# Sign bits of most weight blocks moved from VectorE to ScalarE, and attention blocks ordered earlier, in a fused attention and two-layer kernel

## The chip, the cores and the metric

The kernel runs on one core of one Trainium2 chip. Five engines share the work: TensorE (PE, with its weight loads shown as PEld), VectorE (DVE), ScalarE (ACT), GpSimd (POOL) and SyncE (SP), which here issues all DMAs. The metric is device microseconds (us) of one execution. The kernel before took 1275.98 us in the median of 3 runs (1275.0 to 1279.07).

## What is computed

```
scores = q @ k.T / sqrt(64)                  # 4 batches x 8 heads, 576 x 64 each
keep the 32 largest of each row of 576, softmax over these, attn @ v
x   = rows of the batches, 2304 x 512        # heads side by side
x   = (sigmoid(x @ w_gate) * (x @ w_val)) @ w_out      # 512 -> 1536 -> 512
out = relu(x @ w_in)**2 @ w_out2                       # 512 -> 2048 -> 512
```

q, k and v arrive in float32. All five weights arrive in float64, which no engine computes with: each value is two 32-bit words in SBUF, and the kernel makes a float32 of them by itself.

## The kernel before, in words

The 2304 rows are cut into 18 tiles of 128, and these into 12 chunks (`CHUNKS`): six of one tile, then six of two. For each chunk, attention runs over units: one unit is one tile and one head, with scores on TensorE, a copy `S` to SBUF by ScalarE (L376), four rounds of the eight largest by VectorE (MAX8 L388 and MATCH_REPLACE8 L395), two ScalarE passes for the softmax (L407, L423), a transposition and the product with v. A chunk of one tile has 8 units. Its result is `x_plain` for the first two chunks (L540), which then go through both layers in float32 (`moe32`), straight on the float32 weights. Later chunks use weights and inputs split into two float16 parts.

The weights are worked on while the first attention units run. They come as 68 blocks of 128 x 512 (the names `wg`, `wv`, `wo`, `wi` and `w2`, the last printed as `w` in some rows), two blocks in a step, so 34 steps, each one call of `conv`. For one block of a step: ScalarE copies the high word, taken as float32, times a power of two into `c` (L606); VectorE shifts `c` left by 3, once for both blocks (L620), and ors the sign bit of the high word `hi` into it (L621); ScalarE turns the low word into a small integer in place (L625); and GpSimd adds that integer to `c` (L626). Then the raw block's buffer is free, and SyncE can issue the load of a later block (L579). When the last step of a weight is done, TensorE and VectorE take its scale (L643 to L652).

The order of the work comes from priorities, which a scheduler uses when it lists the instructions of each engine. In the last part of the kernel function two counters are kept: `tw` for weight steps (3 units each, `CW`) and `ta` for attention units (6 units each, `CA`, later 5). The smaller one goes next. `ta` starts at `CA0`. When `x_plain` of a chunk is listed, the body of `moe32` follows, and it forces the weight steps it needs ahead of it. Each engine then works through its list strictly in order.

```python
tw, ta, tm = 0.0, CA0, None
...
            elif tw <= ta and nstep[0] < len(steps):
                at(tw)
                weight_step()
                tw += CW
```

Of the kernel before, what the change touches and what calls it, by code (L numbers as in the profile page):

```python
# [8 lines left out]
F16 = mybir.dt.float16  # L9
BF16 = mybir.dt.bfloat16  # L10
F32 = mybir.dt.float32
F32R = mybir.dt.float32r
I32 = mybir.dt.int32
U32 = mybir.dt.uint32
AF = mybir.ActivationFunctionType
ALU = mybir.AluOpType
# [12 lines left out]
CHUNKS = [[0], [1], [2], [3], [4], [5]] + [[i, i + 1] for i in range(6, 18, 2)]  # L29
AHEAD = 1000  # L30
LEAD = 10
CA0 = -5.0
CA = 6.0
CW = 3.0
SUP = -100.0
# [12 lines left out]
SM2 = ()  # L48
XUP = 1000
DIAG = 2  # L50
SGN = 0
M4RAW = 0
KEYS1 = 1
SWI = 5
# [19 lines left out]
def tile_topk_attention__then__two_moe_layers(  # L74
# [14 lines left out]
    nc = tc.nc  # L89
# [469 lines left out]
    nblk = [0]  # L559
# [5 lines left out]
    def fetch_to(i):  # L565
        while fetched[0] < len(blocks):
            b = fetched[0]
            spare = b >= len(blocks) - M4RAW
            if b > i and not (b <= i + PREF and (spare or live[0] + 3 <= WSLOTS)):
                break  # L570
            n, kt, fb = blocks[b]
            src = weights[n][kt * P : (kt + 1) * P, fb * 512 : (fb + 1) * 512]
            pool, kw = (mpool, {"tag": "m4", "bufs": M4}) if spare else (wpool, {"tag": "w"})
            if src.dtype == F32:
                t = pool.tile([P, 512], F32, name=f"{n}_r{kt}_{fb}", **kw)
                nc.sync.dma_start(t, src)
            else:
                t = pool.tile([P, 512, 2], U32, name=f"{n}_r{kt}_{fb}", **kw)
                nc.sync.dma_start(t.rearrange("p f t -> p (f t)"), src.bitcast(U32))  # L579
            if not spare:  # L580
                live[0] += 1
            raws[(n, kt, fb)] = t
            fetched[0] += 1

    def conv(name, pi):

        pr = pairs_of[name][pi]
        fetch_to(blocks.index((name, *pr[-1])))
        if (name, pi) in CM4:
            c = mpool.tile([P, 2, 512], F32, tag="m4", bufs=M4, name=f"{name}_c{pi}")  # L590
        else:
            c = wpool.tile([P, 2, 512], F32, tag="w", name=f"{name}_c{pi}")
            live[0] += 1
        rs = [raws.pop((name, kt, fb)) for kt, fb in pr]
        ci = c.bitcast(U32)
        wide = weights[name].dtype != F32
        for e, r in enumerate(rs):
            nblk[0] += 1
            if not wide:
                nc.gpsimd.tensor_copy(c[:, e], r)  # L600
            elif YMOD and nblk[0] % YMOD == 0:
                nc.gpsimd.tensor_scalar(
                    c[:, e], r.bitcast(F32)[:, :, 1], REBIAS, 1.0, op0=ALU.mult, op1=ALU.mult
                )
            else:
                nc.scalar.activation(c[:, e], r.bitcast(F32)[:, :, 1], AF.Copy, scale=REBIAS)  # L606
        if wide:
            for e, r in enumerate(rs):
                hi = r[:, :, 1]
                if SGN and nblk[0] % SGN == 0:  # L610

                    nc.gpsimd.tensor_scalar(
                        hi.bitcast(F32), hi.bitcast(F32), 0.0, 1.0, op0=ALU.mult, op1=ALU.mult
                    )
                    nc.vector.scalar_tensor_tensor(
                        ci[:, e], ci[:, e], 3, hi, op0=ALU.logical_shift_left, op1=ALU.bitwise_or
                    )
                else:
                    if e == 0:
                        nc.vector.tensor_scalar(ci, ci, 3, None, op0=ALU.logical_shift_left)  # L620
                    nc.vector.scalar_tensor_tensor(  # L621
                        ci[:, e], hi, 0x80000000, ci[:, e], op0=ALU.bitwise_and, op1=ALU.bitwise_or
                    )
                low = r[:, :, 0].bitcast(I32)
                nc.scalar.activation(low, r[:, :, 0], AF.Copy, scale=float(2.0**-29))  # L625
                nc.gpsimd.tensor_tensor(  # L626
                    c.bitcast(I32)[:, e], c.bitcast(I32)[:, e], low, op=ALU.add
                )
        live[0] -= sum(blocks.index((name, *b)) < len(blocks) - M4RAW for b in pr)
        for e, (kt, fb) in enumerate(pr):  # L630
            flat[(name, kt, fb)] = (c, e)
# [42 lines left out]
    def weight_step(n=1):  # L674
        for _ in range(min(n, len(steps) - nstep[0])):
            name, pi = steps[nstep[0]]
            conv(name, pi)
            nstep[0] += 1
            if name in ("wg", "wv", "wo") and pi == len(pairs_of[name]) - 1:
                scale(name)  # L680
# [508 lines left out]

    tw, ta, tm = 0.0, CA0, None  # L1190
    up[0] = AUP * 50
# [95 lines left out]
```

## Time and profile before

| what | value |
|---|---|
| median of 3 runs | 1275.98 us |
| the profiled execution's own time | 1279.65 us |
| its span, first to last instruction | 1276.8 us |
| PE busy | 1185.2 us, 93% |
| DVE busy | 974.5 us, 76% |
| POOL busy | 848.8 us, 66% |
| ACT busy | 805.8 us, 63% |
| mean granted TensorE clock | 0.959 of full |

Busy time is the time in which an engine had at least one instruction under way. A share over the whole span hides the stages: an engine that is full in one stage and idle in another looks half used. So the stages have to be read apart, by windows of time, and in each the question is which engine was never idle and what the others waited for. Two instructions of one engine can overlap, so what one more costs is the distance between two starts, which is less than its duration.

### The profile page before, as it was taken

The page shows a single profiled execution, that of the slowest core. Times are in us where ns is not written, and L with a number is a line of the kernel's source. Part 1 is how long each engine was busy: PE and PEld are TensorE (multiplying, and loading weights), DVE is VectorE, ACT ScalarE, POOL GpSimd, SP SyncE. Part 2 cuts the span into 40 slices and gives each one's busy share as a digit, 9 for nine tenths or more (in the row PEclk, how much of TensorE's full clock was granted, in tenths as well). Part 3 has the DMA queues.
Part 4 walks back from the last instruction along what each step waited for, and adds up shares of the span by engine and source line. Part 5 has one row for each costly group of instructions (what it writes and reads, how often), then busy time and mean ns, then how long its engine had stood idle before and what let it go on. Part 6 is the DMA issues. An engine that isn't in the chain of part 4 may idle for free.

```text
span 1276.8 us, 30674 instructions
## 1 busy us (share of the span) xinstructions
PE 1185.2 (93%) x11477; PEld 962.5 (75%) x11477; DVE 974.5 (76%) x1989; ACT 805.8 (63%) x1695; POOL 848.8 (66%) x1294
## 2 busy tenths in 40 slices
PE   6757799989899998999998999999999999999998
PEld 5635688887787976878786768877886887787775
DVE  6999989899878968879997789999999969210010
ACT  4876766577767766767766766776676757323122
POOL 1788865477666567786875977798678749515223
PEclk9766899999989989999998999999999999999999
DMA  7977772222444336665566465566444623200000
GB/s 189 347 280 257 265 224 64 73 68 76 135 119 118 89 93 149 140 158 124 125 134 155 115 149 135 120 138 144 113 99 89 129 48 67 55 1 1 17 1 17
DMA packets 243188, 153.92 MB, mean 121 GB/s; under 512 B 193120, under 2 KB 209504, under 8 KB 243040
## 3 DMA queue, kind: packets, MB, share of 16 engines
q1 hardware_dynamic: 243040, 151.97, 46.1%
q8 instruction: 90, 1.47, 0.5%
q14 instruction: 58, 0.48, 0.1%
HBM read 105.51 MB, written 18.09 MB: 97 GB/s over the span
## 4 chain that ended last, share of the span: by engine, by line
PE 58%; DVE 17%; DMA 8%; POOL 6%; issue 5%; ACT 4%; SPq 3%; POOLq 0%; DVEq 0%; ACTq 0%
PE ph L856 11%; PE acc L877 10%; PE pg L752 6%; DVE mx L388 6%; PE pv L752 6%; DVE W L395 6%; PE acc L792 5%; PE sp L373 5%; PE xp L505 2%; PE xp L532 2%; PE ph L957 2%; PE acc L974 2%; DMA PT<-S 2%; POOL S L453 1%; DMA kst<-ks 1%
## 5 line engine op out<-in xcount | busy, mean ns | idle before, releaser
L388 DVE MAX8 mx<-W 128x8 f32<-128x576 f32 x432 | 327.8, 759 | 11.0
L395 DVE MATCH_REPLACE8 W<-mx,W 128x576 f32<-128x576 f32 x288 | 213.8, 742 | 0.0
L856 PE MATMUL ph<-x,wi_w 128*128 128x256 f16 (+1 forms) x1920 | 192.6, 255 | 2.4 <-ACT x L830 1.6
L877 PE MATMUL acc<-w_w,rh 128*128 128x512 f16 x768 | 183.1, 381 | 2.2 <-POOL rh L869 2.2
L856 PEld LDWEIGHTS <-wi_w 128*128 128x128 f16 x1920 | 158.3, 99 | 29.5 <-issue 3.0
L752 PE MATMUL pg<-xs,wg_w 128*128 128x256 f16 (+1 forms) x1440 | 150.8, 253 | 3.2 <-POOL xs L520 1.2
L752 PE MATMUL pv<-xs,wv_w 128*128 128x256 f16 (+1 forms) x1440 | 146.6, 254 | 6.2 <-DVE th L764 5.7
L373 PE MATMUL sp<-kst,qt 128*128 128x288 f32 x608 | 137.1, 336 | 11.1 <-DMA kst<-ks 5.5
L407 ACT ACTIVATE W<-S,mx 128x576 f32<-128x576 f32 x144 | 111.7, 775 | 45.8 <-DVE mx L388 45.3
L453 POOL TENSOR_TENSOR S<-W,S 128x512 f16<-128x512 f32 x192 | 137.0, 736 | 1.5
L376 ACT COPY S<-sp 128x576 f32<-128x576 f32 x144 | 91.7, 637 | 70.0 <-PE sp L373 54.7
L752 PEld LDWEIGHTS <-wv_w 128*128 128x128 f16 x1440 | 119.6, 99 | 20.9 <-issue 7.9
L752 PEld LDWEIGHTS <-wg_w 128*128 128x128 f16 x1440 | 117.8, 99 | 20.7 <-issue 3.5
L792 PEld LDWEIGHTS <-wo_w 128*128 128x128 f16 x1440 | 119.7, 99 | 16.6 <-issue 4.0
L877 PEld LDWEIGHTS <-rh 128*128 128x128 f16 x768 | 72.8, 98 | 73.9 <-POOL rh L869 2.4
L764 DVE TENSOR_TENSOR th<-pv,th 128x512 f32<-128x512 f32 (+1 forms) x60 | 34.5, 575 | 120.6 <-PE pv L752 117.5
L388 DVE MAX8 mx<-S 128x8 f32<-128x576 f32 x144 | 107.2, 744 | 20.2 <-ACT S L376 19.8
L451 POOL TENSOR_SCALAR W<-W,rz 128x576 f32<-128x576 f32 x96 | 71.8, 748 | 66.0 <-ACT S L450 63.2
L373 PEld LDWEIGHTS sp<-kst,qt 128*128 128x128 f32 x608 | 94.0, 198 | 22.2 <-DMA kst<-ks 6.7
L792 PE MATMUL acc<-gh,wo_w 128*128 128x256 f16 (+1 forms) x1104 | 107.8, 252 | 2.7 <-POOL gh L768 2.4
L868 POOL TENSOR_TENSOR r<-r 128x512 f32<-128x512 f32 (+1 forms) x80 | 69.5, 870 | 57.2 <-ACT rh L867 56.6
L395 DVE MATCH_REPLACE8 W<-mx,S 128x576 f32<-128x576 f32 x144 | 106.9, 742 | 0.0
(285 smaller groups left out, 2316.6 us busy)
## 6 DMA issues: line engine op xcount, KB each, us to landing
kst<-ks SPq DMA_DIRECT2D x112, 288.0 KB, 3.1
v<-vd SPq DMA_DIRECT2D x32, 320.0 KB, 3.4
qn<-in_q_dram SPq DMA_DIRECT2D x128, 64.0 KB, 2.4
wi_r<-in_moe_w_in_dram SPq DMA_DIRECT2D x16, 512.0 KB, 7.2
w_r<-in_moe_w_out_dram SPq DMA_DIRECT2D x16, 512.0 KB, 4.3
v<-in_v_dram SPq DMA_DIRECT2D x56, 128.0 KB, 2.3
wg_r<-in_moe_w_gate_dram SPq DMA_DIRECT2D x12, 512.0 KB, 6.3
wv_r<-in_moe_w_val_dram SPq DMA_DIRECT2D x12, 512.0 KB, 7.7
```

Source lines behind the costliest of these rows:

```text
L373: nc.tensor.matmul(sp[:, e, 0:HALF], l, r, start=(x == 0), stop=(x == len(ops) - 1))
L376: nc.scalar.copy(ss.rearrange("p (e s) -> p e s", e=2), sp[:, :, 0:HALF])
L388: m8 = nc.vector.max(mx[:, r], cur)
L395: nc.vector.match_replace(wk, mx[:, r], cur, NEG)
L407: nc.scalar.activation(wk, ss, AF.Prelu, bias=kth, scale=-1.0, alpha=1.0 / BIG)
L451: nc.gpsimd.tensor_scalar(wk, wk, rz, 1.0, op0=ALU.mult, op1=ALU.mult)
L453: nc.gpsimd.tensor_tensor(pp[:, o : o + e - f], wk[:, f:e], pp[:, f:e], op=ALU.subtract)
L752: nc.tensor.matmul(pp[:, e * N : (e + 1) * N], wblk(wd, a, c, f0, P), xs[:, b_, c, :], start=(e == 0 and n == 0), stop=(n == 3 * KM - 1), ...
L792: nc.tensor.matmul(accs[d // 2][:, (d % 2) * N : (d % 2 + 1) * N], wblk("wo", a, f, d * P, P), gh[:, b_, e * N : (e + 1) * N], start=(f == ...
L856: nc.tensor.matmul(ph[:, e * N : (e + 1) * N], wblk("wi", a, c, f0, P), x2[:, b_, c, :], start=(e == 0 and n == 0), stop=(n == 3 * KM - 1) ...
L868: nc.gpsimd.tensor_tensor(r, r, r, op=ALU.mult)
L877: nc.tensor.matmul(acc2[i][:, 0:DM], gh[:, b_, e * N + i * P : e * N + (i + 1) * P], wblk("w2", a, f, 0, DM), start=(f == 0 and x == 0), s ...
```

## The change

Of every three steps, two take another way for the sign. `nblk[0] // 2 % 3` is the step's number, counted from 1, modulo 3, and where it is 0 or 1 ScalarE writes the sign: it multiplies `hi`, taken as float32, by 2 to the power of -60 and stores the result as float16 in the upper half of the low word. The value is too small for float16, so what is stored is a zero with the sign of `hi`, and its one bit is the top bit of the word. The integer add by GpSimd, which is there anyway, carries it into `c`. The or of VectorE is not done in these steps. In the other third it is as before. The shift by VectorE now stands first in the step, and the low word's ScalarE pass stands ahead of the sign.

The second part is one number: `CA0`, from -5 to -15. With 6 units for an attention block, three attention blocks are listed ahead of the first weight step where one was.

```diff
-CA0 = -5.0
+CA0 = -15.0
...
-SGN = 0
+SGN = 3
+SGNS = (0, 1)
...
         if wide:
+            nc.vector.tensor_scalar(ci, ci, 3, None, op0=ALU.logical_shift_left)
             for e, r in enumerate(rs):
                 hi = r[:, :, 1]
-                if SGN and nblk[0] % SGN == 0:
-
-                    nc.gpsimd.tensor_scalar(
-                        hi.bitcast(F32), hi.bitcast(F32), 0.0, 1.0, op0=ALU.mult, op1=ALU.mult
-                    )
-                    nc.vector.scalar_tensor_tensor(
-                        ci[:, e], ci[:, e], 3, hi, op0=ALU.logical_shift_left, op1=ALU.bitwise_or
-                    )
+                low = r[:, :, 0].bitcast(I32)
+                nc.scalar.activation(low, r[:, :, 0], AF.Copy, scale=float(2.0**-29))
+                if nblk[0] // 2 % SGN in SGNS:
+
+                    nc.scalar.activation(
+                        r.bitcast(F16)[:, :, 1], hi.bitcast(F32), AF.Copy, scale=float(2.0**-60)
+                    )
                 else:
-                    if e == 0:
-                        nc.vector.tensor_scalar(ci, ci, 3, None, op0=ALU.logical_shift_left)
                     nc.vector.scalar_tensor_tensor(
                         ci[:, e], hi, 0x80000000, ci[:, e], op0=ALU.bitwise_and, op1=ALU.bitwise_or
                     )
-                low = r[:, :, 0].bitcast(I32)
-                nc.scalar.activation(low, r[:, :, 0], AF.Copy, scale=float(2.0**-29))
                 nc.gpsimd.tensor_tensor(
                     c.bitcast(I32)[:, e], c.bitcast(I32)[:, e], low, op=ALU.add
                 )
```

(The branch with `nc.gpsimd.tensor_scalar` was never taken before, since `SGN` was 0.)

What this does to the lists is seen at three places. In the changed kernel the lines from 51 to the high word's copy stand one further down, and those behind `conv` three further up; the high word's copy is L607, the shift L609, the low word L613, the sign L616 and the or L620 there. A number at the end of a name is a buffer's or a block's.

The first place is VectorE while `wo` is converted and the last unit of the first chunk and the first of the second are searched. Before:

```order
L620 TENSOR_SCALAR wo_c_872<-wo_c_872 128x1024
L388 MAX mx_7_933<-W_7_932 128x8
L621 SCALAR_TENSOR_TENSOR wo_c_872<-wo_r_0_720,wo_c_872 128x512
L621 SCALAR_TENSOR_TENSOR wo_c_872<-wo_r_0_722,wo_c_872 128x512
L428 RECIPROCAL rz_6_789<-bs_6_785 128x1
L620 TENSOR_SCALAR wo_c_954<-wo_c_954 128x1024
L395 MATCH_REPLACE W_7_932<-mx_7_933,W_7_932 128x576
```

Now:

```order
L396 MATCH_REPLACE W_0_974<-mx_0_975,W_0_974 128x576
L389 MAX mx_0_975<-W_0_974 128x8
L609 TENSOR_SCALAR wo_c_996<-wo_c_996 128x1024
L396 MATCH_REPLACE W_0_974<-mx_0_975,W_0_974 128x576
L389 MAX mx_0_975<-W_0_974 128x8
L609 TENSOR_SCALAR wo_c_1032<-wo_c_1032 128x1024
L620 SCALAR_TENSOR_TENSOR wo_c_1032<-wo_r_0_862,wo_c_1032 128x512
L620 SCALAR_TENSOR_TENSOR wo_c_1032<-wo_r_0_864,wo_c_1032 128x512
```

The step on `wo_c_996` has the shift alone, the next one the two ors as before. At this place attention is one unit further than it was. VectorE's list has 1559 rows before and 1513 now, 46 fewer.

The second place is ScalarE around the copy of the fourth head pair's part of `x_plain`, with which the first chunk's input is complete and its first layer can begin. Before, it is row 152 of the list:

```order
L606 ACTIVATE wi_c_1353<-wi_r_0_1152 128x512
L625 ACTIVATE wi_r_0_1152<-wi_r_0_1152 128x512
L606 ACTIVATE wi_c_1353<-wi_r_0_1154 128x512
L625 ACTIVATE wi_r_0_1154<-wi_r_0_1154 128x512
L540 COPY x_plain<-xp_3_1004 128x128
L606 ACTIVATE wi_c_1367<-wi_r_1_1248 128x512
```

Now it is row 186:

```order
L613 ACTIVATE wi_r_1_1250<-wi_r_1_1250 128x512
L607 ACTIVATE wi_c_1479<-wi_r_1_1349 128x512
L613 ACTIVATE wi_r_1_1349<-wi_r_1_1349 128x512
L607 ACTIVATE wi_c_1479<-wi_r_1_1351 128x512
L541 COPY x_plain<-xp_3_962 128x128
L613 ACTIVATE wi_r_1_1351<-wi_r_1_1351 128x512
L616 ACTIVATE wi_r_1_1248<-wi_r_1_1248 128x512
L172 CAST kp_1_1047<-kpt_1_0_1048 128x512
```

The 34 more rows ahead of it are 29 signs (L616), four copies of high words of `wi` and one softmax pass of a later unit.

The third place is ScalarE around the first Relu of the first chunk's second layer, `r_0`. Before, it is row 258:

```order
L474 COPY PT_5_1969<-tp_5_1970 128x512
L483 COPY PE_2_1918<-tq_5_1976 64x128
L423 ACTIVATE W_6_1991,bs_6_2000<-W_6_1991,bs_6_2000 128x576
L625 ACTIVATE w_r_0_1829<-w_r_0_1829 128x512
L966 ACTIVATE r_0_1868<-ph_0_1859 128x256
L606 ACTIVATE w_c_1831<-w_r_0_1817 128x512
```

Now it is row 310:

```order
L947 COPY x_plain<-acc_0_1318 128x512
L658 ACTIVATE wv_w_2533<-wv_c_668,wvs 128x1024
L424 ACTIVATE W_6_1991,bs_6_2000<-W_6_1991,bs_6_2000 128x576
L377 COPY S_0_2125<-sp_0_2126 128x576
L541 COPY x_plain<-xp_2_1979 128x128
L658 ACTIVATE wg_w_2536<-wg_c_361,wgs 128x1024
L963 ACTIVATE r_0_1868<-ph_0_1859 128x256
```

The 52 more rows ahead of it are all 46 signs, two copies of high words, three float16 splits of weights (L658) and one copy of a part of `x_plain`. Attention stands at the same unit in both lists.

## Rows read from the trace of the kernel before

**Rows 1.** Busy us of each engine by windows of the span (first column: window in us).
```profile
core 0: us, PE busy (x) PEld busy (x) DVE busy (x) ACT busy (x) POOL busy (x), PEclk, DMA share, GB/s
0.00:40.00 40.00, 29.86 (x122) 22.71 (x122) 25.06 (x51) 20.68 (x44) 8.08 (x19) 1.00 0.77 226
40.00:160.00 120.00, 80.43 (x529) 65.27 (x529) 118.31 (x204) 89.96 (x179) 103.32 (x87) 0.73 0.81 281
...
195.00:327.00 132.00, 128.80 (x1048) 107.32 (x1047) 121.84 (x227) 92.16 (x185) 81.34 (x124) 1.00 0.27 75
327.00:440.00 113.00, 104.81 (x1394) 92.56 (x1392) 94.83 (x200) 78.62 (x181) 76.08 (x139) 0.92 0.42 117
440.00:700.00 260.00, 240.69 (x2918) 201.55 (x2916) 221.19 (x494) 180.71 (x419) 187.71 (x339) 0.96 0.58 131
700.00:1200.00 500.00, 496.30 (x4644) 389.68 (x4642) 358.87 (x747) 300.50 (x611) 344.65 (x541) 1.00 0.41 92
```

**Rows 2.** Timeline of ScalarE at two places (start us, us busy, engine, line, what).
```profile
119.64 0.27 ACT L540 COPY x_plain<-xp 128x128 f32<-128x128 f32 x1
...
194.67 0.38 ACT L966 ACTIVATE r<-ph 128x256 f32<-128x256 f32 x1
...
196.61 1.15 ACT L661 ACTIVATE wg_w<-wg_c,wgs 128x1024 f16<-128x1024 f32 x1
197.66 0.26 ACT L540 COPY x_plain<-xp 128x128 f32<-128x128 f32 x1
```

**Rows 3.** Busy us by windows that end at these two places.
```profile
40.00:119.64 79.64, 49.08 (x304) 36.88 (x303) 78.02 (x132) 60.08 (x118) 67.82 (x56) 0.68 0.83 293
119.64:194.67 75.03, 64.44 (x522) 58.31 (x523) 69.88 (x133) 55.13 (x113) 60.11 (x57) 0.91 0.75 239
```

**Rows 4.** Groups of VectorE's ors, 0 to 300 us (count, busy us, mean ns, idle before).
```profile
L621 DVE SCALAR_TENSOR_TENSOR w_c<-w_r,w_c 128x512 uint32<-128x512 uint32 x16 | 12.9, 843 | 0.0
L621 DVE SCALAR_TENSOR_TENSOR wi_c<-wi_r,wi_c 128x512 uint32<-128x512 uint32 x16 | 12.3, 807 | 0.0
L621 DVE SCALAR_TENSOR_TENSOR wv_c<-wv_r,wv_c 128x512 uint32<-128x512 uint32 x12 | 10.4, 906 | 0.0
L621 DVE SCALAR_TENSOR_TENSOR wg_c<-wg_r,wg_c 128x512 uint32<-128x512 uint32 x12 | 9.0, 788 | 0.0
L621 DVE SCALAR_TENSOR_TENSOR wo_c<-wo_r,wo_c 128x512 uint32<-128x512 uint32 x12 | 8.9, 781 | 0.0
```

**Rows 5.** Timeline of ScalarE, back to back, around 131 us.
```profile
129.84 0.58 ACT L474 COPY PT<-tp 128x512 f32<-128x512 f32 x1
130.31 0.70 ACT L606 ACTIVATE wi_c<-wi_r 128x512 f32<-128x512 f32 x1
...
131.04 0.69 ACT L625 ACTIVATE wi_r<-wi_r 128x512 int32<-128x512 uint32 x1
131.61 0.67 ACT L606 ACTIVATE wi_c<-wi_r 128x512 f32<-128x512 f32 x1
132.16 0.68 ACT L625 ACTIVATE wi_r<-wi_r 128x512 int32<-128x512 uint32 x1
132.73 0.37 ACT L345 CAST qt<-qpt 128x256 fp32r<-128x256 f32 x1
```

**Rows 6.** GpSimd's adds and VectorE's ors by line (ns min/median/max, first and last start us).
```profile
L626 POOL TENSOR_TENSOR wv_c<-wv_c,wv_r x12: 1286/1712/1751, 65.2 to 88.5; 128x512 int32<-128x512 int32 x12
...
L621 DVE SCALAR_TENSOR_TENSOR wv_c<-wv_r,wv_c x12: 668/682/1782, 64.5 to 86.7; 128x512 uint32<-128x512 uint32 x12
```

**Rows 7.** What ScalarE waited for, 40 to 195 us (total us, times, longest).
```profile
ACT S L376 <- PE sp L373: 10.0, 8, 2.9
ACT PT L474 <- PE tp L471: 8.1, 4, 2.6
ACT W L407 <- DVE mx L388: 6.7, 6, 1.9
ACT W L423 <- POOL bs L404: 3.9, 3, 1.7
```

## The prediction

> **What bounds the kernel now.** I read the busy time by windows first, because the whole span says only that TensorE is the busiest [rows 1]. From 40 to 160 us VectorE is busy for 118.31 of 120 us, while TensorE has 80.43, at a granted clock of 0.73 of full, ScalarE 89.96 and GpSimd 103.32. So the front of the kernel runs at VectorE's pace. From 195 us on TensorE is the full one: 128.80 of 132 us, and 496.30 of 500 us from 700 to 1200. Between 327 and 700 us it is idle for 8.19 and 19.31 us. What comes out of the front earlier or later is therefore handed on to the end nearly whole, since TensorE has the same work behind it.
>
> Two marks cut the front. At 119.64 us ScalarE copies the last part of the first chunk's input, and its first layer can begin on TensorE; at 194.67 us the first Relu of its second layer starts [rows 2]. The lists show that at the second mark attention stands at the same unit before and now, so whatever this mark is moved by, the rest is moved by. Between 40 us and the first mark VectorE is 98% busy (78.02 of 79.64) and ScalarE 60.08; between the marks VectorE has 69.88 of 75.03, TensorE 64.44 and ScalarE 55.13 [rows 3]. I start at 40 us because ahead of it the first weight blocks are only arriving, and the lists differ little there.
>
> **What is removed.** 46 ors of VectorE, of 68. The 68 take 53.5 us together (sum of five groups), 0.787 us each, so 46 are 36.2 us [rows 4]. The shifts stay, one for each step, 34 in both lists. If VectorE alone set the pace, this would be the gain.
>
> **What is added.** 46 passes of ScalarE over 128x512 values with a stride. The trace has no such pass with a float16 output; the nearest rows are the two passes over the same words: starts 0.57, 0.55 and 0.57 us apart when back to back [rows 5]. I take 0.57, so 26.2 us. The lower end is the 128x512 copy from PSUM, 0.47 us from start to start, which gives 21.6 us; the upper end is the full duration of 0.68 us with no overlap, 31.3 us [rows 5].
>
> **What is moved.** Ahead of the first mark ScalarE's list has 34 more rows, which at 0.57 us are 19.4 us (one of them, a softmax pass, is a little longer). Ahead of the second it has 52 more: 46 signs, 26.2 us; two copies of high words, 1.1 us; three splits at 1.05 us (196.61 to 197.66), 3.2 us; one small copy, 0.2 us [rows 2]. Together 30.7 us, so 11.3 us of it between the marks. The splits and copies are work done earlier, not more work. GpSimd has the same 68 adds, and 3 more rows ahead of its step behind the second mark. SyncE issues 808 DMAs in both, with the weight loads now behind a few more attention loads at the very front; the DMA engines are 0.83 busy up to the first mark [rows 3], so there is room for this, but not much. TensorE's list up to the second layer has 10 more small products and is otherwise the same.
>
> **The sum.** ScalarE's work from 40 us to the first mark becomes 60.08 + 19.4 = 79.5 us in a stretch that took 79.64; between the marks it becomes 55.13 + 11.3 = 66.4 of 75.03 [rows 3]. So ScalarE takes VectorE's place. VectorE falls to some 118 of 154.67 us (147.9 less 44 ors in the stretch at 0.787, plus a few moved rows), GpSimd stays near 128, and TensorE at 64.44 between the marks cannot be passed there either. How full ScalarE gets decides. I give it the 98% that VectorE had up to the first mark: 79.5 / 0.98 = 81.1 us, 1.5 us more than before, and 66.4 / 0.98 = 67.8 us, 7.3 us less. The second mark then comes 5.8 us earlier, and so does the end: 1279.65 - 5.8 = 1273.9 us for an execution like the profiled one, and against the median of the runs, which is 3.7 us below it, 1270 us. Of the 36 us that leave VectorE nearly all are given back as the new engine's load.
>
> The late stages cost nothing in this sum. TensorE's idle time from 327 to 700 us is 27.5 us in many small waits [rows 1]; the lists are shuffled there too, and I allow 4 us to either side.
>
> **The rivals.** With 145.9 us of ScalarE's work in a stretch of 154.67, its busy share s gives everything: the shift is 145.9 / s - 154.67. It is zero at 94.3%, a gain of 3.8 us (0.3%, about what runs of this kernel can tell from no change) at 96.7%, and a loss of as much at 92%.
>
> *No change that can be told*, s between 92 and 96.7%. Both halves do what is said and balance. For it: ScalarE does not choose its work, and its list mixes conversions with attention; its waits now are on three other engines [rows 7]. Against: most of these waits fall where VectorE or a TensorE at half clock is late, and ScalarE, being late itself, will find the operands there. Time 1276 us.
>
> *Slower: ScalarE's list stops at its head.* Each copy of scores that waits for TensorE (10.0 us now), each transposed tile (8.1 us), each maximum (6.7 us) holds up the conversions queued behind it, and these hold up GpSimd's adds, the raw buffers and the next loads [rows 7]. Should it keep half of today's 39.5 us of idle time, s is 145.9 / (145.9 + 19.7) = 88%, the second mark comes 11 us later, and the time is 1287 us. The place is the first stretch, where ScalarE has no room at all; the point from which it decides is 92%. The trace bears it out in part: ScalarE was 74% busy in this stretch, 115.2 of 154.67 us [rows 3]. The Trainium skill speaks on this side: its page "ScalarE: Activation LUTs", in "Rules for kernel authors", puts multiplications and the like on VectorE and not on ScalarE. The rows here say the reverse of the single instruction, 0.57 us against 0.787 [rows 4, 5], and leave the rule its point only through the queue. That page's "What ACT_TABLE_LOAD costs" also states a price, 186 ns and 0.833 ns for each element, less an overlap of 93 ns: an estimate of 0.52 us for a sign, by which the sum would be some 8 us of gain; the trace's spacing is longer, and is used.
>
> *More gain: relief of GpSimd.* Its adds take 1.29 us at best and 1.71 in the median of `wv`, and single ors 1.78 us instead of 0.68 [rows 6]: these two get in each other's way. With 46 ors gone, both get shorter, up to 0.4 us for an add, the sign reaches the adds sooner, and less of ScalarE's idle time is GpSimd's doing. With the sign at the lower price too, 141.3 us at 98% is a gain of 10.5 us, and some us in the late waits make 12 to 16. The Trainium skill's page "SBUF — State Buffer", in "SBUF: two separate sides", states that a VectorE instruction with two SBUF inputs and a GpSimd one that reads SBUF exclude each other; these rows agree. GpSimd is not the full engine in the new balance, so the sum itself gets nothing from it.
>
> *The change does nothing* is excluded: the lists show 46 rows gone from VectorE and 46 new on ScalarE.
>
> **How the numbers follow.** The forecast, s from 96.7 to 98.5%, has 0.40, the larger gain 0.05, no change 0.30, slower 0.25. So faster by over 0.3% has 0.45. The range goes from a gain of 16 us, 1260, to the loss of 11 us, 1287. The likeliest alone would lie between 1266 and 1273.
>
> **What would show it.** In the changed trace the ors number 22 and the signs 46, of about 0.68 us and 0.57 us from start to start. ScalarE should be over 95% busy between 40 us and the second mark, VectorE near 80%, and the Relu `r_0` should start near 189 us, with the input copy ahead of the first layer near 121 us. GpSimd's adds should have a median nearer 1.3 us. From there on the shift should stay the same to the end. The prediction is wrong if ScalarE is under 92% busy there, if the sign costs more than 0.68 us, if TensorE's second layer starts earlier without an earlier end, or if the shift arises behind 327 us and not in the front.

## The result, and the profile after

The changed kernel takes 1285.48 us in the median of 5 runs (1282.52 to 1286.47), the kernel before 1275.98 us in 5 runs on the same chip (1275.0 to 1279.07). The ratio is 1.007, with an interval from 1.0054 to 1.0086: 0.7% slower, where 0.5% faster was forecast. Of all runs behind this document one, of experiment 4, was far slower than the rest (2334.75 us) and is left out of its ratio. The profiled executions are single ones: the one of the kernel before took 1279.65 us, the one of the changed kernel 1285.48.

The busy times of the changed kernel by windows, in the columns of [rows 1]:

```profile
core 0: us, PE busy (x) PEld busy (x) DVE busy (x) ACT busy (x) POOL busy (x), PEclk, DMA share, GB/s
...
40.00:160.00 120.00, 77.79 (x480) 62.58 (x481) 89.75 (x154) 119.76 (x199) 85.45 (x82) 0.65 0.79 271
...
195.00:327.00 132.00, 128.16 (x1031) 107.95 (x1030) 117.40 (x221) 94.01 (x182) 80.94 (x120) 1.00 0.30 82
327.00:440.00 113.00, 103.03 (x1307) 88.99 (x1306) 93.79 (x194) 77.44 (x184) 77.17 (x135) 0.94 0.43 120
440.00:700.00 260.00, 240.70 (x3037) 201.81 (x3035) 224.15 (x500) 181.69 (x423) 189.24 (x345) 0.99 0.61 131
700.00:1200.00 500.00, 495.23 (x4621) 387.59 (x4620) 364.94 (x759) 303.46 (x622) 345.99 (x546) 1.00 0.43 92
```

Read the line from 40 to 160 us against the one of before. The full engine of the front has changed: VectorE falls from 118.31 to 89.75 of 120 us, ScalarE rises from 89.96 to 119.76. Behind 327 us the lines differ by little. The two marks of [rows 2] now stand here, in ScalarE's timeline:

```profile
130.03 0.26 ACT L541 COPY x_plain<-xp 128x128 f32<-128x128 f32 x1
...
207.44 0.88 ACT L963 ACTIVATE r<-ph 128x256 f32<-128x256 f32 x2
```

They come 10.4 and 12.8 us later than before, and so the busy times up to them, as in [rows 3]:

```profile
40.00:130.03 90.03, 53.95 (x306) 40.13 (x305) 67.88 (x115) 89.83 (x150) 62.80 (x60) 0.57 0.82 285
130.03:207.44 77.41, 63.78 (x539) 57.85 (x540) 56.19 (x111) 76.31 (x132) 50.25 (x54) 0.96 0.68 206
```

ScalarE is busy for 166.14 of the 167.44 us, 99%. Its idle time, 39.5 us before, is 1.3 us, and these are all the waits that the profile lists for it between 40 and 207 us (total us, times, longest):

```profile
ACT w_c L607 <- POOL w_c L623: 0.4, 1, 0.4
ACT PT L475 <- PE tp L472: 0.2, 1, 0.2
ACT w_r L613 <- DMA w_r<-in_moe_w_out_dram: 0.2, 1, 0.2
```

So ScalarE's list did not stop at its head. It had more to do: 166.1 us of work up to the second mark, where the sum had 145.9. The groups of the sign passes (ns min/median/max, first and last start) tell why:

```profile
L616 ACT ACTIVATE wi_r<-wi_r x10: 1335/1362/1473, 121.5 to 150.2; 128x512 f16<-128x512 f32 x10
L616 ACT ACTIVATE wv_r<-wv_r x8: 1342/1370/1388, 63.2 to 92.4; 128x512 f16<-128x512 f32 x8
```

One sign takes 1.36 us and not 0.68. What it costs is the distance to the next start, and the timeline shows that beside the other passes:

```profile
117.03 0.74 ACT L607 ACTIVATE wi_c<-wi_r 128x512 f32<-128x512 f32 x1
117.60 0.73 ACT L613 ACTIVATE wi_r<-wi_r 128x512 int32<-128x512 uint32 x1
118.14 1.42 ACT L616 ACTIVATE wo_r<-wo_r 128x512 f16<-128x512 f32 x1
119.22 0.79 ACT L607 ACTIVATE wi_c<-wi_r 128x512 f32<-128x512 f32 x1
...
120.37 1.42 ACT L616 ACTIVATE wo_r<-wo_r 128x512 f16<-128x512 f32 x1
121.46 1.47 ACT L616 ACTIVATE wi_r<-wi_r 128x512 f16<-128x512 f32 x1
```

From 117.03 to 117.60 a high word costs 0.57 us; from 120.37 to 121.46 a sign costs 1.09. Over the 44 signs with no gap behind them the median is 1.087 us. Forty-six times the excess of 0.52 is 24 us, which covers the 20.2 us by which the work came out larger than the sum.

To follow a shift through the kernel I use one more measure, TensorE's progress. Each matmul gets, as its weight, the median distance to the next start that its shape has in the kernel before; the shift at t is how much earlier (-) or later (+) than before the sum of weights reached at t is reached. It counts work in whatever order it is done. Other ways to weigh the shapes move its figures by about 1 us. In the changed kernel it is +9.6 at 300 us, +9.3 at 800 and +8.2 at 1000, and the last instruction ends 6.4 us later (span 1283.2 us against 1276.8): made in the front, and in the main handed on.

### The profile page after: what moved, and what is told of

Same layout as the page of the kernel before. It is cut to its first block, busy times and chain, and to the rows that moved or that the text cites. A ratio compares the mean times of both kernels' runs of the same rounds, so it can differ in the third digit from the quotient of the medians.

```text
span 1283.2 us, 30671 instructions
## 1 busy us (share of the span) xinstructions
PE 1177.7 (92%) x11477; PEld 954.8 (74%) x11477; DVE 945.5 (74%) x1943; ACT 852.8 (66%) x1741; POOL 832.8 (65%) x1294
## 4 chain that ended last, share of the span: by engine, by line
PE 55%; ACT 14%; DVE 13%; DMA 7%; POOL 5%; issue 3%; SPq 2%; DVEq 0%; POOLq 0%; ACTq 0%
PE ph L853 11%; PE acc L874 10%; PE pv L749 6%; PE pg L749 6%; PE acc L789 5%; DVE mx L389 5%; DVE W L396 5%; PE sp L374 4%; PE ph L954 2%; PE xp L506 2%; DMA PT<-S 2%; PE acc L971 2%; PE xp L533 2%; PE pg L907 2%; DMA kst<-ks 1%
## 5 line engine op out<-in xcount | busy, mean ns | idle before, releaser
L749 PE MATMUL pg<-xs,wg_w 128*128 128x256 f16 (+1 forms) x1440 | 148.0, 254 | 5.1 <-ACT xs L520 2.9
L749 PE MATMUL pv<-xs,wv_w 128*128 128x256 f16 (+1 forms) x1440 | 145.8, 254 | 6.3 <-DVE th L761 4.9
L374 PE MATMUL sp<-kst,qt 128*128 128x288 f32 x608 | 134.0, 331 | 15.1 <-DMA kst<-ks 8.2
L749 PEld LDWEIGHTS <-wv_w 128*128 128x128 f16 x1440 | 118.5, 99 | 23.0 <-issue 10.1
L749 PEld LDWEIGHTS <-wg_w 128*128 128x128 f16 x1440 | 118.6, 99 | 18.9 <-issue 3.0
L789 PEld LDWEIGHTS <-wo_w 128*128 128x128 f16 x1440 | 117.5, 98 | 13.9 <-issue 2.0
L789 PE MATMUL acc<-gh,wo_w 128*128 128x256 f16 (+1 forms) x1104 | 104.1, 247 | 1.6 <-ACT gh L764 1.5
L451 ACT ACTIVATE S<-W,rz 128x576 f16<-128x576 f32 x96 | 74.4, 775 | 45.1 <-DVE rz L447 44.7
```

What stands on the lines that cost most here:

```text
L374: nc.tensor.matmul(sp[:, e, 0:HALF], l, r, start=(x == 0), stop=(x == len(ops) - 1))
L451: nc.scalar.activation(pp[:, 0:S], wk, AF.Copy, scale=rz)
L749: nc.tensor.matmul(pp[:, e * N : (e + 1) * N], wblk(wd, a, c, f0, P), xs[:, b_, c, :], start=(e == 0 and n == 0), stop=(n == 3 * KM - 1), ...
L789: nc.tensor.matmul(accs[d // 2][:, (d % 2) * N : (d % 2 + 1) * N], wblk("wo", a, f, d * P, P), gh[:, b_, e * N : (e + 1) * N], start=(f == ...
```

## The experiments

Three theories at first, by the letters that the expectations use. **A, price:** the sign passes are dear because of how they store, and at 0.57 us the prediction's sum would have held. **B, queue:** conversions in front of attention in ScalarE's list do harm whatever a sign costs. **C, order:** the loss comes from the new order number.

**1. The sign as a whole word.** Only the output of L616 differs; the lists of all engines are identical to the changed kernel's.

```diff
-                        r.bitcast(F16)[:, :, 1], hi.bitcast(F32), AF.Copy, scale=float(2.0**-60)
+                        low, hi.bitcast(F32), AF.Copy, scale=float(2.0**-60)
```

> The sign pass stores a 4-byte integer zero over the low word instead of a 2-byte float16 into its upper half; every list of instructions is the same as in the changed kernel. (Two thirds of the weight blocks are then left without their signs and low words.) Theory A, the price of the narrow store: the pass falls from 1.09 to 0.57 us between starts, 46 x 0.52 = 24 us leave ScalarE in the front, the Relu r_0 moves from 207.4 to between 184 and 191 us (TensorE's own work ends the gain), and the time is 1264 to 1272 us. Theory B, the queue: ScalarE as the pace engine holds up attention whatever the pass costs; ScalarE shows waits of 15 us or more between 40 and 195 us, and the time stays above 1279 us. Theory C, the order number: nothing that depends on the pass; the time stays at 1285 us.

Measured: 1263.15 us (6 runs), ratio 0.9911 (0.9889 to 0.9934), 22 us below the changed kernel. The sign row and the window:

```profile
L616 ACT ACTIVATE wi_r<-wi_r x10: 663/689/722, 108.4 to 131.9; 128x512 int32<-128x512 f32 x10
```

```profile
40.00:185.80 145.80, 114.35 (x840) 96.65 (x840) 123.39 (x224) 140.65 (x277) 116.03 (x113) 0.74 0.84 285
```

The sign is 0.69 us long and 0.566 from start to start. `r_0` stands at 185.8 us, 8.8 us earlier than before, with ScalarE 140.65 of 145.8 us busy. The time is 1 us below the range of A. ScalarE's waits from 40 to 195 us add up to 7 us, where B had 15 or more, and C's 1285 us did not come. With the instructions in the same order, the store alone is worth 22 us: price, and not the queue.

**2. The same float16, side by side.** Is it the type or the step?

```diff
-                        r.bitcast(F16)[:, :, 1], hi.bitcast(F32), AF.Copy, scale=float(2.0**-60)
+                        r.bitcast(F16).rearrange("p f t -> p (f t)")[:, 0:512], hi.bitcast(F32), AF.Copy, scale=float(2.0**-60)
```

> The sign pass reads the same words and still stores float16, but 512 values side by side in place of one in every 8 bytes. (The raw block is overwritten, so low words and signs of two thirds of the blocks are left out; the lists are shuffled by the other dependency.) If the price lies in the 2-byte store with a step (theory A), the pass takes 0.67 to 0.72 us, 0.57 between starts. If it lies in the conversion to float16 or in the zeros, it stays at 1.35 us.

One run, 1262.27 us; the start-to-start distance is 0.569 us. Float16 itself costs nothing, so it is the step:

```profile
L616 ACT ACTIVATE wi_r<-wi_r x10: 643/660/677, 108.8 to 134.0; 128x512 f16<-128x512 f32 x10
```

**3. Each part alone.** First the changed kernel with the number of before, then the kernel before with the number of the change.

```diff
-CA0 = -15.0
+CA0 = -5.0
```

```diff
-CA0 = -5.0
+CA0 = -15.0
```

> The signs by ScalarE as in the change, with CA0 back at -5. A and B: ScalarE is full as before, 1283 to 1289 us. C: the loss goes with the order number, 1273 to 1278 us.

> The kernel before with CA0 at -15 and nothing else. A and B: VectorE still sets the pace with the same work, 1272 to 1280 us. C: the loss is here, 1282 us or more.

The sign alone: 1300.88 us (4 runs), ratio 1.0197 (1.0173 to 1.0222), worse than any theory had it. ScalarE is full here too:

```profile
40.00:120.00 80.00, 49.63 (x277) 36.81 (x276) 59.02 (x105) 79.86 (x132) 55.20 (x52) 0.85 0.85 294
120.00:160.00 40.00, 24.11 (x153) 21.02 (x154) 25.80 (x50) 39.93 (x69) 30.76 (x30) 0.70 0.72 233
```

The order alone: 1286.86 us (6 runs), ratio 1.0099 (1.0073 to 1.0124). That is a miss for A and B and lies in C's range, which the sign alone and experiment 1 missed. So the number does harm by itself, but it is not what the change lost by. The front is earlier here, `r_0` by 10.2 us, and yet the end is later. TensorE's progress is -5.9 us at 300, -18.6 at 500 and +7.2 at 800, so the loss arises between 500 and 800 us. Windows there, of the kernel before, then of this one:

```profile
500.00:800.00 300.00, 285.18 (x3190) 234.83 (x3188) 259.87 (x565) 208.12 (x468) 227.63 (x394) 0.98 0.60 138
```

```profile
500.00:800.00 300.00, 271.24 (x2914) 220.21 (x2912) 252.85 (x549) 204.13 (x454) 221.27 (x380) 0.96 0.62 133
```

And the waits of TensorE there that grew most, before and here (`PT` are attention's transposed weights, `kst` its keys):

```profile
PE sp L373 <- DMA kst<-ks: 3.1, 2, 1.9
...
PE xp L505 <- DMA PT<-S: 2.8, 3, 1.3
```

```profile
PE xp L505 <- DMA PT<-S: 9.0, 4, 3.8
PE sp L373 <- DMA kst<-ks: 6.7, 3, 3.4
```

TensorE had run ahead in the layers (`th`, the first pass behind the gate's product, starts 18.9 us earlier for the fifth chunk) while attention had not: counting units from 0, the first maximum of unit 16 is 0.9 us earlier, that of unit 56 3.1. TensorE then stood more, 13.9 us of the 25.8 lost between 500 and 800, and what it waited longer for are mostly attention's operands. So the trace reads as work done early that attention could not follow. No run tested it. Of the other 12 us some 6 are an estimate for the granted clock, 0.96 instead of 0.98 in these windows; the rest is not accounted for.

**4. Fewer dear signs.** One step in three by ScalarE, 22 signs.

```diff
-SGNS = (0, 1)
+SGNS = (0,)
```

> The changed kernel with one step in three by ScalarE instead of two: 22 signs at 1.09 us are 24 us, about what the prediction had put down for 46. A: ScalarE is 94 to 98% busy between 40 us and r_0, r_0 starts at 187 to 193 us, the time is 1267 to 1275 us. B: half of the loss remains, 1279 to 1283 us.

1277.2 us (12 runs), ratio 1.0016 (1.0 to 1.0033), between the theories. `r_0` is 14.1 us earlier, more than A had, unit 16 only 5.7. TensorE's progress goes from -10.3 us at 300 and -16.2 at 500 to +0.9 at 800: the gain of the front is lost at the same place as in the order alone.

**5. The cheap sign without the order.** Experiment 1 with `CA0 = -5`. Its lists are those of the sign alone in 3.

```diff
-CA0 = -15.0
+CA0 = -5.0
```

> The word store of e1 with CA0 back at -5: what the order number is worth when the sign pass is cheap. If the number matters only where ScalarE's list is full to the end of the front, as the runs of the parts suggest, this is within 6 us of the 1263 us of e1; if attention has to be listed early in any case, it loses 15 us again, about 1278 us.

1274.02 us (12 runs), ratio 0.9996 (0.9978 to 1.0015). The expectation had at most 1269 us or about 1278, and neither came. With the dear sign the order number takes 1.3% off (1.0197 to 1.007), with the cheap one 0.85% (0.9996 to 0.9911); on the kernel before it adds 1%. The price is worth 2.0% at -5 and 1.6% at -15, each time between two kernels with the same lists (1.0197 to 0.9996, and 1.007 to 0.9911). So the parts of the change do not add up: of these three pairs, the number pays in the two where ScalarE has taken the signs. Why is not shown.

**6. A sign that VectorE merges with its shift.** ScalarE writes the sign as a whole float32 zero over the high word, and VectorE shifts and ors in one pass for each block; in two of three steps, then in one of three.

```diff
+                    nc.scalar.activation(hi.bitcast(F32), c[:, e], AF.Copy, scale=float(2.0**-60))
...
+                    nc.vector.scalar_tensor_tensor(
+                        ci[:, e], ci[:, e], 3, hi, op0=ALU.logical_shift_left, op1=ALU.bitwise_or
```

> A version with the right result: in two steps of three ScalarE makes the signed zero from c as a 4-byte float32 in place of the high word, and VectorE shifts and ors in one instruction. ScalarE gets 46 x 0.57 = 26 us, as the prediction had it; VectorE loses only 46 x 0.52 = 24 us (23 shifts of 1.04) instead of 36. If ScalarE's price is all that was wrong (theory A), the front comes near that of the word store: Relu r_0 at 183 to 192 us and 1264 to 1273 us. If attention's pace through VectorE counts for the end as well, it is between one step in three and the word store: 1268 to 1275 us. Slower than before if the queue rival holds.

> The same with one step in three: ScalarE gets 22 x 0.57 = 12.5 us, VectorE loses 22 x 0.52 = 11.5 us. VectorE remains the fuller engine, about 136 us of the 155. A: some gain, 1269 to 1277 us. If attention's marks decide, less than e7 gains.

The signs come out missing in these steps, as explained in 7, so they are read for the time alone. 1282.44 us (7 runs), ratio 1.0056 (1.0035 to 1.0078), and 1284.56 us (7 runs), ratio 1.0068 (1.0044 to 1.0093): misses. The signs are cheap (0.66 us long, 0.55 from start to start), but VectorE's 46 passes take 47.4 us in the first, where 36 were reckoned with, the price of as many ors. Two of their five groups, and the window, of the first of the two kernels:

```profile
L619 DVE SCALAR_TENSOR_TENSOR wi_c<-wi_c,wi_r 128x512 uint32<-128x512 uint32 x10 | 12.3, 1241 | 0.0
L619 DVE SCALAR_TENSOR_TENSOR wo_c<-wo_c,wo_r 128x512 uint32<-128x512 uint32 x8 | 11.7, 1489 | 0.0
```

```profile
40.00:120.00 80.00, 46.27 (x307) 35.33 (x307) 75.78 (x124) 78.19 (x153) 68.46 (x60) 0.67 0.91 322
```

VectorE (75.78 of 80) and ScalarE (78.19) are both nearly full, and nothing is won: `r_0` is 1.6 us later than before. By its expectation a slower kernel spoke for the queue, but with VectorE's price missed as well, this run does not separate the two. In the second kernel `r_0` is 9.0 us earlier, and the gain is lost behind it.

**7. A step of 4 bytes.** The low words' integers are stored side by side, in the front half of the block, and the float16 zero into their upper halves; it reads `c`, and VectorE's shift waits for it.

```diff
+                    low = r.rearrange("p f t -> p (f t)")[:, 0:512].bitcast(I32)
...
+                    nc.scalar.activation(
+                        low.bitcast(F16).rearrange("p (f t) -> p f t", t=2)[:, :, 1],
+                        c[:, e], AF.Copy, scale=float(2.0**-60),
+                    )
```

> As the changed kernel, but in two of three steps ScalarE stores the low word's integer side by side (512 words of 4 bytes, step 4 bytes) instead of in place (step 8), and the float16 zero with the sign goes into the upper half of these words, so its store has a step of 4 bytes instead of 8. It reads c instead of the high word, and VectorE's shift waits for it. GpSimd's add then reads its second input side by side. Nothing is left out. If any 2-byte store with a step pays twice, the sign takes 1.35 us again, 1.09 from start to start, ScalarE is full again up to the second layer and the time is 1280 to 1290 us. If only the step of 8 bytes is dear, the sign takes 0.65 to 0.70 us, and the time is 1262 to 1270 us, near the two runs with cheap signs, and this would be a version that beats both kernels.

> The run with side-by-side words again, with the sign pass's factor 1 instead of 2 to the power of -60: the high word's copy is already 2 to the power of -112 of its value, and a product too small for float32 came out without its sign. With the factor 1 nothing is left out. The factor costs no time, so 1277 to 1283 us again, ratio about 1.002.

1280.1 us (10 runs), ratio 1.0024 (1.0008 to 1.004); with the factor 1 for the sign, 1279.07 us (10 runs), 1.0025 (1.0008 to 1.0042). In the first, signs are left out; the factor is the only difference between the two, so its products, which are too small for float32, must have lost the sign on the way. That the two take the same time also speaks against the weights' values setting it, so the kernels that leave signs or low words out can be read for theirs; low words were not tried apart. The sign row of the second:

```profile
L618 ACT ACTIVATE wi_r<-wi_c x10: 762/779/793, 112.0 to 136.8; 128x512 f16<-128x512 f32 x10
```

0.78 us long, 0.634 from start to start: nearer the cheap price than the dear one. But the time is a miss: with a cheap sign 1262 to 1270 us was expected. TensorE's progress is -10.1 us at 180 us and -0.1 at 225, and stays between -0.1 and -6.1 up to 650; so the gain of the front is gone before the second layer is well under way. (This kernel's profiled execution is the slowest of its ten, 1287.47 us.)

**8. The order number in that kernel.** -21 and -10 instead of -15. The letters stand for two new theories here.

```diff
-CA0 = -15.0
+CA0 = -21.0
...
+CA0 = -10.0
```

> As the exact run with side-by-side words, with the order number at -21 instead of -15: one more attention unit ahead. Theory A, the end follows the mark of the attention units behind the front, which one more unit ahead brings forward: 1270 to 1277 us. Theory B, the front's gain is taken back between units 40 and 136 by how the later lists fall, which the number does not govern: 1277 to 1287 us.

> As the exact run with side-by-side words, with the order number at -10 instead of -15, between the two numbers of the change. Theory A: 1279 to 1286 us, since attention is later. Theory B: anywhere from 1270 to 1287 us, without order between the three numbers.

1276.31 us, ratio 1.0019 (1.0003 to 1.0035), and 1279.6 us, ratio 1.0036 (1.0016 to 1.0056), 10 runs each. The intervals of the three numbers overlap, but nine of the ten runs with -21 lie at 1278.01 us or less, where one and two of ten do with -15 and -10: some 3 us for -21 are likely. Both times lie in theory A's ranges, the first just outside B's. The mark does not bear A out, though: unit 16 starts 16.9, 20.6 and 18.3 us earlier than before with -15, -21 and -10, earlier with -10 than with -15, and no end is earlier than before. By unit 24, at 258 us before, attention's lead is down to 1.0, 0.9 and 3.7 us.

The traces show what did not come earlier: the last weight. GpSimd's last adds of `w2` (`w_c`) end at 202.8 us before and 183.2 in experiment 1, but at 201.9, 202.5 and 200.4 with -15, -21 and -10. Before, in experiment 1, and with -21:

```profile
199.28 3.54 POOL L626 TENSOR_TENSOR w_c<-w_c,w_r 128x512 int32<-128x512 int32 x2
```

```profile
181.88 1.31 POOL L623 TENSOR_TENSOR w_c<-w_c,w_r 128x512 int32<-128x512 int32 x1 [1.16 <-ACT w_r L616]
```

```profile
200.03 2.49 POOL L629 TENSOR_TENSOR w_c<-w_c,w_r 128x512 int32<-128x512 int32 x2
```

The products for the scale of `w2` (`w_n`) wait for these adds and hold up what stands behind them in TensorE's list. TensorE's window, before and with -21, and its longest wait in the latter:

```profile
190.00:205.00 15.00, 15.00 (x148) 12.58 (x149) 12.95 (x23) 10.94 (x21) 10.23 (x10) 1.00 0.34 103
```

```profile
190.00:205.00 15.00, 5.54 (x30) 3.17 (x30) 9.28 (x15) 11.14 (x19) 9.62 (x13) 0.70 0.22 64
PE w_n L646 <- POOL w_c L629: 8.1, 4, 6.6
```

With -15 and -10 TensorE is busy for 12.1 of these 15 us. So `r_0` was the wrong mark for these kernels: it came 4.2, 12.0 and 5.6 us earlier while the weights did not. No run tested this.

**TensorE's progress in all of them** (us against the kernel before, worked out as above from one profiled execution each, so that a row can be some us off its kernel's median; the ratio is from the timed runs):

```
                       300     500     800    1000   ratio
changed kernel        +9.6    +6.8    +9.3    +8.2   1.0070
1 whole word         -11.9   -16.9   -14.4   -15.6   0.9911
2 side by side       -12.5   -17.8   -14.5   -14.7   (one run)
3 sign alone         +14.6   +17.5   +24.1   +22.2   1.0197
3 order alone         -5.9   -18.6    +7.2    +4.8   1.0099
4 one in three       -10.3   -16.2    +0.9    -0.7   1.0016
5 whole word, -5      -9.0   -12.8    -2.5    -3.8   0.9996
6 merged, 2 of 3      +0.2    -3.4    +5.3    +3.6   1.0056
6 merged, 1 of 3      -7.2    +0.3   +11.8    +8.4   1.0068
7 step of 4, factor 1 -1.6    -2.5    +7.1    +7.5   1.0025
8 the same, -21       -1.2    -4.7    +1.0    -0.8   1.0019
8 the same, -10       -4.3   -10.2     0.0    -0.6   1.0036
```

What a kernel has at 800 us it still has at 1000, to 4 us. What it has at 300 the changed kernel and experiments 1 and 2 keep, also to 4 us; the others lose 3 to 16 us by 1000 (the one with -21, which had little, 0.4), and between 500 and 800 us alone up to 26. Two pairs have the same lists: the changed kernel and 1 move by -1.4 and -3.7 us from 300 to 1000, the sign alone and 5 by +7.6 and +5.2. So in these pairs the loss goes with the lists and not with how early the front ends. The two kernels of experiment 7 have the same lists as well; the one that is not in the table has -3.3 us at 300 and +2.0 at 1000. For the order alone the waits point to TensorE being ahead of attention. In 7 and 8 little of a gain was left by 300 us (-1.2 to -4.3), with `w2` as late as before. Where attention was ahead as well and `w2` was early (5), it is not settled which rows of the lists lose the time. No version here that writes the signs beats the kernel before.

## Why the prediction was wrong

**What held.** The bottleneck of the front moved from VectorE to ScalarE, as said. ScalarE was 99% busy up to the second mark; over 95% was forecast. VectorE fell to 124.07 of 167.44 us, 74%, where "near 80%" was said, the stretch being longer. GpSimd's adds got quicker, from a median of 1712 ns [rows 6] to 1297:

```profile
L623 POOL TENSOR_TENSOR wv_c<-wv_c,wv_r x12: 1283/1297/1733, 64.6 to 93.8; 128x512 int32<-128x512 int32 x12
```

In the change itself the shift of the front was in the main handed on, as said: 12.8 us at the second mark, +9.6 at 300 us, +8.2 at 1000, and 9.5 between the medians. The time lies inside the stated range of 1260 to 1287 us, on the side that was given 0.25.

**The step that failed** is "What is added": "I take 0.57, so 26.2 us", with "the upper end is the full duration of 0.68 us". The signs cost 1.087 us each, 50 us in all; "if the sign costs more than 0.68 us" was among the prediction's own signs of being wrong. The nearest rows were picked by what they read, the same words with the same step; the sign differs from them in what it writes, 2 bytes every 8. The range of the price had no row behind it that wrote so, and its upper end should have lain as far as a factor of two. Put into the prediction's own sum, 24 us more work gives 169.9 us; at 99% that is 171.6 us for a stretch that took 154.67, 16.9 us more and not the 12.8 measured, so the sum was some 4 us too heavy elsewhere. Of these, 2.5 us are work that ScalarE did ahead of 40 us, where it was busy for 20.68 us before [rows 1] and now 23.20:

```profile
0.00:40.00 40.00, 26.00 (x124) 19.52 (x125) 26.02 (x54) 23.20 (x46) 8.52 (x21) 0.98 0.76 226
```

Experiment 1 is the kernel whose price the prediction described, with 0.566 us for a sign. Its second mark came 8.8 us earlier and its end 12.3 us, where 5.8 was forecast: the forecast's side, at the size of the "more gain" rival, but not by its lower price. ScalarE was 96% busy and not 98%, and the stretch held 140.65 us of its work and not 145.9; the rest of the gain came behind the second mark.

The sum had no term for the order number either. By itself it costs 1% (experiment 3), and with the signs on ScalarE it gains 0.85 to 1.3%. That is not what turned the forecast: with the number and the cheap sign the kernel is faster (0.9911).

**The slower rival** named the right sign for a wrong reason. It let ScalarE keep idle time, with a busy share under 92%; its idle time went from 39.5 us to 1.3. That its 1287 us lies near the measured 1285.48 is luck. That the waits would vanish once ScalarE is the late one, which the prediction held against that rival, is what happened.

**The Trainium skill's price.** The Trainium skill's page "ScalarE: Activation LUTs", in "What ACT_TABLE_LOAD costs", led to an estimate of 0.52 us for a sign. The runs come within 10% of it for a whole word or for float16 side by side (0.566 and 0.569), and not for the 2-byte store with a step of 8 bytes (1.087); the measurement decides.

**Handing on, in general.** "What comes out of the front earlier or later is therefore handed on to the end nearly whole" was true of the change and of experiments 1 and 2, to 4 us from 300 us on. In nearly all other lists 3 to 16 us were lost again between 300 and 1000 us. That the second mark moves the rest with it failed more plainly as a rule: with the second mark 10.2 us earlier the order alone ended later. The prediction allowed 4 us to either side for the shuffled lists there; the runs show that this term can be larger than the whole effect forecast.

## What to carry to other kernels

Price a pass by its output as well as its input: width and step of the store belong to the shape, and a row that shares only the read is not the nearest row. Where a change makes another engine the full one, its price per instruction decides the sign of the result, so double it once in the working and see whether the forecast turns. And a gain at one mark of the front did not reach the end here where attention, or the last weight, did not come earlier with it: follow the progress of the engine that is full at the end, and of what it will wait for, not one mark.

## What the runs showed of the hardware

- ScalarE's 128x512 pass from float32 costs, from start to start, 0.566 us with a 4-byte store every 8 bytes, 0.569 with float16 side by side, 0.634 with float16 every 4 bytes and 1.087 with float16 every 8 bytes. (The third reads side by side, the others every 8 bytes.) Why the last is dear is not shown.
- A product of ScalarE that is too small for float32 came out as a zero without its sign (factor 2 to the power of -60 on `c`, which is already 2 to the power of -112 of its value); one that is only too small for float16 kept it (the same pass with the factor 1). This is from comparing the two kernels of experiment 7, and was not tried apart.
- VectorE's or of two SBUF operands beside GpSimd's adds goes from 0.68 us up to 1.78 [rows 6]; in experiment 6 a group of the merged pass averages 1.49 us. No add that takes less than 1.34 us overlaps an or in the kernel before.
